# Attention queries transposed by VectorE from 32 by 32 blocks in SBUF, keys still by TensorE

## The chip, the cores and the metric

One core of one Trainium2 chip. The metric is the device time in microseconds of one execution. "Time" below is the median of some executions; each profile is of one of them, and its span is about 2 us shorter than its time. "Fast" is the usual state of an execution.

## The reference

Two stages, cut to what matters. 64 heads of attention with a threshold, then one feed-forward layer over the joined heads:

```python
# q, k, v: (8, 8, 576, 64) float32; tau = 0.02
scores = q @ k.T / 8                                  # per head, 576 x 576
thresh = max(scores, -1) - tau
scores = where(scores >= thresh, scores, -1e9)
attn = softmax(scores)
x = (attn @ v), heads joined                          # (4608, 512)
h = x @ w_in                                          # (4608, 2048)
g = h * clip(h + 3, 0, 6) / 6
out = g @ w_out                                       # (4608, 512) float32
```

## The kernel before

A main loop of 16 quads (four heads, as two pairs) times nine slots. A slot is 128 query rows of two heads. PSUM is the memory that TensorE's results go to here, SBUF the one that the operands are kept in; to evict is to copy a result from PSUM to SBUF, which makes the PSUM buffer free for its next user. In the same slots run the feed-forward matmuls of earlier batches. Heads of a pair stand one below the other, 64 partitions each, so scores need queries and keys as [2 x 64, 576]; both are brought there by transposes.

```python
ps_s = psum_pool(bufs=2)   # scores      ps_h = psum_pool(bufs=1)  # x @ w_in
ps_o = psum_pool(bufs=1)   # g @ w_out   ps_m = psum_pool(bufs=1)  # transposes AND attn @ v

def transpose_main(pair, i):                       # i = 0: queries, 1: keys
    main = nat[pair // 2][i][0]
    ps = ps_m.tile([P, 512], F32, tag="m", name="tp")
    for t in range(4):
        nc.tensor.transpose(ps[:, t * P:(t + 1) * P], main[:, t, 2 * (pair % 2):2 * (pair % 2) + 2, :], identf[:])
    def evict():
        if i == 0:
            nc.scalar.activation(out=qkT[pair][0][:, 0:512], in_=ps[:], func=Act.Copy, scale=scale)
        else:
            nc.scalar.copy(out=qkT[pair][1][:, 64:576], in_=ps[:])
    return evict
# ... transpose_rest: the last 64 rows of q and k, the same way, in four small transposes

def av_main(pair):                                 # attn @ v for 512 rows: the same ps_m
    ps = ps_m.tile([P, 512], F32, tag="m", name="av")
    # ... ten matmuls
    nc.vector.tensor_copy(out=xT[b][:, hp, o0:o0 + 512], in_=ps[:])
```

The order of issue in one slot follows. In the traces the engines take up their work in this order:

```python
        sm_exp(prev, 0); sm_exp(prev, 1)           # ScalarE, the slot before
        sm_max(sl)                                 # VectorE: 2 passes over the scores; GpSimd: bias
        if slot != 8 and todo1:
            h = mm1(i, j)                          # TensorE
            r = mm1_relu(h, on_act=(slot in (0, 3)))   # ScalarE in two slots, VectorE in the others
            mm1_gate(i, j, h, r)                   # VectorE, waits for r
        sm_recip(prev)                             # VectorE
        # ... some of the g @ w_out matmuls, evicted by VectorE
        sm_mask(sl, 0); sm_mask(sl, 1)             # ScalarE
        if slot in (1, 2):    evict = transpose_main(2 * quad + 1, slot - 1)
        elif slot == 3:       av_main(2 * quad - 1)        # if quad > 0
        elif slot == 4:       av_rest(quad - 1)            # if quad > 0
        elif slot in (5, 6):  evict = transpose_main(nxt, slot - 5)
        elif slot == 7:       evict = transpose_rest((nxt, nxt + 1))
        elif slot == 8:       av_main(2 * quad)
        if evict: evict()                          # ScalarE, behind the slot's two masks
        queue[n + 1].tiles = scores(...)           # TensorE
        sm_norm(prev)                              # GpSimd, then a DMA transpose of the probabilities
```

## Time and profile before

| | before |
|---|---|
| median time | 592.41 us (592.33 to 594.22, 3 runs) |
| first reciprocal of VectorE | 15.6 us |
| first four quads together | 123.2 us (30.8 each) |
| the next eleven quads | 32.97 us each |
| TensorE busy, 60 to 90 us / 300 to 350 us | 25.15 of 30 / 50.00 of 50 |

The quads are timed by VectorE's reciprocals in the trace: nine a quad, one a slot, and the distance from the first of one quad to the first of the next is that quad's pace. This divides the span into a start, an early part in which the feed-forward work has hardly begun (its ReLUs start at 87 us), a middle, and a tail. The lines of the profile are in the prediction below.

### The profile page before, as it was taken

To read this page: it belongs to the slowest core of one execution; us is meant where nothing else is said; L and a number is where in the kernel's file an instruction comes from. 1 tells how busy PE (TensorE), PEld (TensorE's weight loads), DVE (VectorE), ACT (ScalarE), POOL (GpSimd) and SP (SyncE) were. 2 spreads that over 40 slices of the span, in tenths; PEclk is the share of its full clock that TensorE was granted. 3 is DMA by queue.
4 is the path that set the end of the run, shared out by engine and by line. 5 is a ranking of instruction groups with operands and counts; after the bars stand their busy time and mean duration, and the time that the engine had idled before them with its cause. 6 is when DMAs were issued, how large, how long until landed. Compare 5 with 4: busy or idle time off the path is not lost. (4 is left out here: it accounts for less than half of the span.)

```text
span 589.8 us, 11554 instructions
## 1 busy us (share of the span) xinstructions
PE 552.3 (94%) x3840; PEld 319.8 (54%) x3840; DVE 412.4 (70%) x1008; ACT 480.0 (81%) x1078; POOL 305.5 (52%) x646
## 2 busy tenths in 40 slices
PE   6887698889999999999999999999999999999997
PEld 3544354545556555656556565655556565554663
DVE  1545467777878887888868787888868787872350
ACT  4999899798889898898878988898879989881340
POOL 0769676875555555654555555654555555550000
PEclk9978689989999999999999999999999999999999
DMA  5999999999697768976697758985698746552101
GB/s 116 142 178 191 180 152 192 163 177 154 132 154 150 154 119 152 152 155 137 140 137 155 151 119 163 141 162 126 133 138 158 153 101 108 97 110 69 54 19 71
DMA packets 269498, 80.45 MB, mean 136 GB/s; under 512 B 252544, under 2 KB 264832, under 8 KB 269440
## 3 DMA queue, kind: packets, MB, share of 16 engines
q1 hardware_dynamic: 252032, 70.81, 63.4%
q0 software_dynamic: 17408, 8.92, 13.5%
q8 instruction: 30, 0.49, 0.4%
q14 instruction: 28, 0.23, 0.1%
HBM read 36.70 MB, written 9.44 MB: 78 GB/s over the span
## 5 line engine op out<-in xcount | busy, mean ns | idle before, releaser
L230 POOL TENSOR_SCALAR pn<-s,rinv 128x576 bf16<-128x576 f32 x288 | 211.6, 745 | 143.8 <-issue 89.3
L210 DVE TENSOR_SCALAR_CACHE_REDUCE s<-s 128x576 f32<-128x576 f32 x288 | 206.7, 755 | 86.6 <-PE s L189 69.1
L218 ACT ACTIVATE s<-s,bias 128x576 f32<-128x576 f32 x288 | 207.3, 767 | 56.1 <-POOL bias L213 55.3
L222 ACT ACTIVATE s<-s 128x576 f32<-128x576 f32 x288 | 192.9, 672 | 0.4
L189 PE MATMUL s<-kT,qT 64*128 64x288 f32 x1024 | 178.2, 450 | 3.4 <-DVE s L210 2.3
L274 PE MATMUL h<-xT,w_in_sb 128*128 128x288 bf16 x1024 | 144.6, 287 | 3.5 <-DVE g L290 2.8
L302 PE MATMUL o<-w_out_sb,g 128*128 128x512 bf16 x576 | 139.9, 379 | 3.9 <-DVE osb L310 3.9
L274 PEld LDWEIGHTS <-w_in_sb 128*128 128x128 bf16 x1024 | 91.6, 98 | 65.8 <-issue 21.1
L189 PEld LDWEIGHTS s<-kT,qT 64*128 64x128 f32 x1024 | 98.6, 195 | 49.7 <-DVE s L210 12.8
L290 DVE SCALAR_TENSOR_TENSOR g<-r,h 128x576 bf16<-128x576 f32 x128 | 96.5, 754 | 26.1 <-ACT r L282 23.3
L213 POOL TENSOR_SCALAR bias<-m 128x1 f32<-128x1 f32 x288 | 54.6, 190 | 79.0 <-DVE s L210 58.3
L302 PEld LDWEIGHTS <-g 128*128 128x128 bf16 x576 | 55.6, 98 | 59.6 <-issue 9.9
L284 DVE TENSOR_SCALAR r<-h 128x576 f32<-128x576 f32 x81 | 61.0, 753 | 0.0
L222 ACT ACTIVATION_READ_ACCUMULATOR s<-s 128x1 f32 x288 | 54.4, 189 | 0.0
L282 ACT ACTIVATE r<-h,three 128x576 f32<-128x576 f32 x47 | 34.5, 736 | 12.3 <-PE h L274 11.8
L245 PE MATMUL av<-pT,vm 128*64 128x512 bf16 x256 | 36.0, 405 | 8.0 <-ACT kT L174 6.3
L310 DVE TENSOR_SCALAR osb<-o 128x512 f32<-128x512 f32 x30 | 20.3, 678 | 29.3 <-PE o L302 28.6
L245 PEld LDWEIGHTS <-vm 128*64 128x64 bf16 x512 | 20.3, 112 | 33.5 <-issue 26.8
L225 DVE RECIPROCAL rinv<-rsum 128x2 f32<-128x2 f32 x144 | 23.0, 160 | 21.2 <-ACT s L222 20.8
L308 ACT ACTIVATE osb<-o 128x512 f32<-128x512 f32 x6 | 3.6, 597 | 30.4 <-PE o L302 30.4
L152 PE MATMUL tp<-identf,km 128*128 128x128 f32 x128 | 20.9, 288 | 7.1 <-ACT qT L156 7.1
L258 DVE CAST xT<-av 128x512 bf16<-128x512 f32 x32 | 21.8, 682 | 6.3 <-PE av L249 6.3
(32 smaller groups left out, 270.5 us busy)
## 6 DMA issues: line engine op xcount, KB each, us to landing
qm<-in_q_dram SPq DMA_DIRECT2D x64, 128.0 KB, 3.1
km<-in_k_dram SPq DMA_DIRECT2D x64, 128.0 KB, 3.0
out_dram<-osb SPq DMA_DIRECT2D x32, 256.0 KB, 2.6
vm<-in_v_dram POOLq DMA_DIRECT2D x16, 256.0 KB, 5.9
pT<-pn SPq DMA_TRANSPOSE x128, 3.5
w_in_sb<-in_moe_w_in_dram POOLq DMA_DIRECT2D x16, 128.0 KB, 4.1
w_out_sb<-in_moe_w_out_dram POOLq DMA_DIRECT2D x16, 128.0 KB, 3.6
qr<-in_q_dram SPq DMA_DIRECT2D x16, 64.0 KB, 2.7
```

What stands on the lines that cost most here:

```text
L189: nc.tensor.matmul(tiles[a][:, hf, 0:HALF], qkT[pair][0][a * 64:(a + 1) * 64, t * P:(t + 1) * P], keys(pair, a, hf), start=True, stop=True)
L210: nc.vector.tensor_scalar(out=sl.s[:, i, :].rearrange("p (a b) -> p a b", a=2), in0=ps[:, :, 0:HALF], scalar1=1.0, scalar2=None, op0=Alu.m ...
L213: nc.gpsimd.tensor_scalar(out=sl.bias[:, i:i + 1], in0=sl.m[:, i:i + 1], scalar1=-1.0, scalar2=tau, op0=Alu.mult, op1=Alu.add)
L218: nc.scalar.activation(out=s, in_=s, func=Act.Prelu, bias=sl.bias[:, i:i + 1], alpha=REJECT)
L222: nc.scalar.activation(out=s, in_=s, func=Act.Exp, accum_out=sl.rsum[:, i:i + 1])
L230: nc.gpsimd.tensor_scalar(out=pn[:, i, :], in0=sl.s[:, i, :], scalar1=sl.rinv[:, i:i + 1], scalar2=1.0, op0=Alu.mult, op1=Alu.mult)
L245: nc.tensor.matmul(ps[a * 64:(a + 1) * 64, :], vm[:, 2 * hp + a, c * D:(c + 1) * D], pT[:, 5 * a + c, cols], start=(c == 0), stop=False)
L274: nc.tensor.matmul(hps[:, hf, 0:HALF], w_in_sb[:, ki, ni * P:(ni + 1) * P], xT[b][:, ki, hf * HALF:(hf + 1) * HALF], start=(ki == 0), stop ...
L282: nc.scalar.activation(out=r[:], in_=hps[:, :, 0:HALF], func=Act.Relu, bias=three[:])
L284: nc.vector.tensor_scalar(out=r[:], in0=hps[:, :, 0:HALF], scalar1=3.0, scalar2=0.0, op0=Alu.add, op1=Alu.max)
L290: nc.vector.scalar_tensor_tensor(out=g.rearrange("p (a b) -> p a b", a=2), in0=r[:], scalar=6.0, in1=hps[:, :, 0:HALF], op0=Alu.min, op1=A ...
L302: nc.tensor.matmul(o_ps[0], gbuf[:, ni, mt * P:(mt + 1) * P], w_out_sb[:, ni, :], start=(ni == 0), stop=(ni == NI - 1))
```

## The change

Intent: take 160 transposes of the queries and their evictions off TensorE and ScalarE. Each 32-wide half of a head is loaded on its own 32 partitions, so that VectorE's transposition of 32 by 32 blocks gives the wanted layout, from SBUF to SBUF. The scale of 1/8 goes from the eviction into the mask, and ScalarE takes over two more ReLUs a quad from VectorE. Query rows are in plain order now, so the rows of the output are too. The diff, with the change of the loops' bookkeeping cut:

```diff
     def load_quad(quad):
+        nat[quad] = (nat_pool.tile([P, 2, 18, 32], F32, tag="nq", name="nq"),
+                     nat_pool.tile([P, 4, 4, D], F32, tag="km", name="km"), ...)
+        def main_q(n, a, j):
+            c = 32 * (2 * a + j)
+            nc.sync.dma_start(out=nat[quad][0][c:c + 32, n, :, :],
+                              in_=q[b, 4 * g + 2 * n + a, :, 32 * j:32 * j + 32].rearrange("(k r) d -> r k d", r=32))
@@
+    def transpose_q(pair):
+        nc.vector.transpose(out=qkT[pair][0][:], in_=nat[pair // 2][0][:, pair % 2, :, :].rearrange("p k d -> p (k d)"))
+    def transpose_k(pair):      # as transpose_main with i = 1
@@ transpose_rest
-            for i in range(2):
-                nc.tensor.transpose(ps[:, (2 * n + i) * 64:(2 * n + i + 1) * 64], ...)
+            nc.tensor.transpose(ps[:, n * 64:(n + 1) * 64], nat[pair // 2][2][:, 2 * n:2 * n + 2, :], identf[:64, :64])
@@ sm_max, sm_mask
-            ... bias: scalar1=-1.0, scalar2=tau
+            ... bias: scalar1=-scale, scalar2=tau
-        nc.scalar.activation(out=s, in_=s, func=Act.Prelu, bias=sl.bias[:, i:i + 1], alpha=REJECT)
+        nc.scalar.activation(out=s, in_=s, func=Act.Prelu, bias=sl.bias[:, i:i + 1], scale=scale, alpha=REJECT)
@@ mm2_out
-        return [(osb[:], out[r0:r0 + 512, :].rearrange("(p t) n -> p t n", t=4)[:, t, :])]
+        return [(osb[:], out[r0 + t * P:r0 + (t + 1) * P, :])]
@@ main loop
-            r = mm1_relu(h, on_act=(slot in (0, 3)))
+            r = mm1_relu(h, on_act=(slot in (0, 1, 3, 5)))
-        if slot in (1, 2):
-            evict = transpose_main(2 * quad + 1, slot - 1)
+        if slot == 1:
+            transpose_q(2 * quad + 1)
+        elif slot == 2:
+            evict = transpose_k(2 * quad + 1)
@@ slot 5
-            evict = transpose_main(nxt, slot - 5) if slot < 7 else transpose_rest((nxt, nxt + 1))
+                transpose_q(nxt)
+            elif slot == 6:
+                evict = transpose_k(nxt)
+            else:
+                evict = transpose_rest((nxt, nxt + 1))
```

More of the change, by code (lines that the diff above doesn't have):

```diff
@@ L76, in load_quad, with main_k, rest @@
         b, g = divmod(quad, 2)
-        nat[quad] = []
-        for nm in "qk":
-            nat[quad].append((nat_pool.tile([P, 4, 4, D], F32, tag=nm + "m", name=nm + "m"),
-                              nat_pool.tile([64, 4, D], F32, tag=nm + "r", name=nm + "r")))
-        def main(i, h):
-            src = (q, k)[i]
-            nc.sync.dma_start(out=nat[quad][i][0][:, :, h, :],
-                              in_=src[b, 4 * g + h, 0:512, :].rearrange("(p t) d -> p t d", t=4))
-        def rest(i):
-            src = (q, k)[i]
-            nc.sync.dma_start(out=nat[quad][i][1][:],
-                              in_=src[b, 4 * g:4 * g + 4, 512:S, :].rearrange("h p d -> p h d"))
+        nat[quad] = (nat_pool.tile([P, 2, 18, 32], F32, tag="nq", name="nq"),
+                     nat_pool.tile([P, 4, 4, D], F32, tag="km", name="km"),
+                     nat_pool.tile([64, 4, D], F32, tag="kr", name="kr"))
+        def main_q(n, a, j):
+            c = 32 * (2 * a + j)
+            nc.sync.dma_start(out=nat[quad][0][c:c + 32, n, :, :],
+                              in_=q[b, 4 * g + 2 * n + a, :, 32 * j:32 * j + 32].rearrange("(k r) d -> r k d", r=32))
+        def main_k(h):
+            nc.sync.dma_start(out=nat[quad][1][:, :, h, :],
+                              in_=k[b, 4 * g + h, 0:512, :].rearrange("(p t) d -> p t d", t=4))
+        def rest():
+            nc.sync.dma_start(out=nat[quad][2][:],
+                              in_=k[b, 4 * g:4 * g + 4, 512:S, :].rearrange("h p d -> p h d"))
         for n in range(2):
-            for i in range(2):
-                loads.append(lambda n=n, i=i: [main(i, 2 * n + a) for a in range(2)])
+            loads.append(lambda n=n: [main_k(2 * n + a) for a in range(2)])
+            loads.append(lambda n=n: [main_q(n, a, j) for a in range(2) for j in range(2)])
             if n == 0:
-                loads.append(lambda: [rest(i) for i in range(2)])
+                loads.append(rest)
     def load_v(b):
@@ L146, in alloc_qk @@
                      qk_pool.tile([P, S + 64], F32, tag="kT", name="kT"))
-    def transpose_main(pair, i):
-        main = nat[pair // 2][i][0]
+    def transpose_q(pair):
+        nc.vector.transpose(out=qkT[pair][0][:], in_=nat[pair // 2][0][:, pair % 2, :, :].rearrange("p k d -> p (k d)"))
+    def transpose_k(pair):
         ps = ps_m.tile([P, 512], F32, tag="m", name="tp")
         for t in range(4):
-            nc.tensor.transpose(ps[:, t * P:(t + 1) * P], main[:, t, 2 * (pair % 2):2 * (pair % 2) + 2, :], identf[:])
-        def evict():
-            if i == 0:
-                nc.scalar.activation(out=qkT[pair][0][:, 0:512], in_=ps[:], func=Act.Copy, scale=scale)
-            else:
-                nc.scalar.copy(out=qkT[pair][1][:, 64:576], in_=ps[:])
-        return evict
+            nc.tensor.transpose(ps[:, t * P:(t + 1) * P],
+                                nat[pair // 2][1][:, t, 2 * (pair % 2):2 * (pair % 2) + 2, :], identf[:])
+        return lambda: nc.scalar.copy(out=qkT[pair][1][:, 64:576], in_=ps[:])
     def transpose_rest(pairs):
@@ L163, in transpose_rest @@
         for n, pair in enumerate(pairs):
-            for i in range(2):
-                nc.tensor.transpose(ps[:, (2 * n + i) * 64:(2 * n + i + 1) * 64],
-                                    nat[pair // 2][i][1][:, 2 * n:2 * n + 2, :], identf[:64, :64])
+            nc.tensor.transpose(ps[:, n * 64:(n + 1) * 64], nat[pair // 2][2][:, 2 * n:2 * n + 2, :], identf[:64, :64])
         def evict():
             for n, pair in enumerate(pairs):
-                qT, kT = qkT[pair]
-                src = ps[:, 2 * n * 64:(2 * n + 1) * 64], ps[:, (2 * n + 1) * 64:(2 * n + 2) * 64]
-                nc.scalar.activation(out=qT[:, 512:S], in_=src[0], func=Act.Copy, scale=scale)
-                nc.scalar.copy(out=kT[0:64, S:S + 64], in_=src[1][0:64, :])
-                nc.scalar.copy(out=kT[64:P, 0:64], in_=src[1][64:P, :])
+                kT = qkT[pair][1]
+                nc.scalar.copy(out=kT[0:64, S:S + 64], in_=ps[0:64, n * 64:(n + 1) * 64])
+                nc.scalar.copy(out=kT[64:P, 0:64], in_=ps[64:P, n * 64:(n + 1) * 64])
         return evict
@@ L212, in sm_max @@
                                     accum_out=sl.m[:, i:i + 1])
-            nc.gpsimd.tensor_scalar(out=sl.bias[:, i:i + 1], in0=sl.m[:, i:i + 1], scalar1=-1.0, scalar2=tau,
+            nc.gpsimd.tensor_scalar(out=sl.bias[:, i:i + 1], in0=sl.m[:, i:i + 1], scalar1=-scale, scalar2=tau,
                                     op0=Alu.mult, op1=Alu.add)
@@ L217, in sm_mask @@
         s = sl.s[:, i, :]
-        nc.scalar.activation(out=s, in_=s, func=Act.Prelu, bias=sl.bias[:, i:i + 1], alpha=REJECT)
+        nc.scalar.activation(out=s, in_=s, func=Act.Prelu, bias=sl.bias[:, i:i + 1], scale=scale,
+                             alpha=REJECT)
     def sm_exp(sl, i):
@@ L332 @@
     alloc_qk(1)
-    for i in range(2):
-        transpose_main(0, i)()
+    transpose_q(0)
+    transpose_k(0)()
     transpose_rest((0, 1))()
```

## The prediction

> **What bounds the kernel now.** I read the engines' busy shares first, then stretches of the span, then the waits of the long middle part, and last the order of time within single slots. (A slot is one pass of the main loop, 128 query rows of two heads; nine slots make a quad of four heads; there are 16 quads.) The engines, and TensorE's row and granted clock over 40 slices:
>
> ```profile
> PE 552.3 (94%) x3840; PEld 319.8 (54%) x3840; DVE 412.4 (70%) x1008; ACT 480.0 (81%) x1078; POOL 305.5 (52%) x646
> ...
> PE   6887698889999999999999999999999999999997
> ...
> PEclk9978689989999999999999999999999999999999
> ```
>
> TensorE is full from the tenth slice on and not before; there its clock is also reduced. The stretches show the same with numbers (columns: stretch, length, then busy us of PE, PEld, DVE, ACT, POOL, clock, DMA share, GB/s):
>
> ```profile
> 60.00:90.00 30.00, 25.15 (x152) 14.20 (x151) 16.45 (x49) 27.04 (x63) 19.79 (x43) 0.77 1.05 166
> ...
> 300.00:350.00 50.00, 50.00 (x374) 29.62 (x374) 41.13 (x100) 42.95 (x96) 26.35 (x57) 1.00 0.77 136
> ```
>
> So there are two regimes and a tail: quads 0 to 3 (to about 140 us), where ScalarE is busiest and TensorE waits; quads 4 to 15 (to 530 us), where TensorE does nothing but work; and about 60 us of feed-forward matmuls alone, which the change does not touch. A busy TensorE need not be a limiting one, so I asked who waits for whom between 165 and 500 us:
>
> ```profile
> PE o L302 <- DVE osb L310: 3.7, 5, 1.4
> ...
> ACT s L218 <- POOL bias L213: 38.5, 56, 2.2
> ...
> DVE s L210 <- PE s L189: 39.8, 57, 2.4
> ```
>
> In 335 us TensorE waits 4.3 us in all (the row shown and one of 0.6), while VectorE waits 39.8 us for TensorE's scores and ScalarE 38.5 us for what follows from them. This middle is TensorE's, and what is taken off TensorE there shortens it. The pace is read from the once-per-quad transpose of the leftover probabilities:
>
> ```profile
> 137.78 1.51 SPq L237 DMA_TRANSPOSE pR<-pn  x1
> ...
> 498.93 1.30 SPq L237 DMA_TRANSPOSE pR<-pn  x1
> ```
>
> Eleven quads in 361.2 us are 32.8 us each; the three before took (137.8 - 43.0)/3 = 31.6 us.
>
> [...] The new load puts each 32-wide half of a head on its own 32 partitions, so that blocks are enough and no eviction follows. [...] I estimate 0.75 us. The trace agrees for passes of that size (753 to 755 ns for 128x576 in f32), but no transpose is in it. [...] in the 0.77 stretch a slot's eight score matmuls took 2.29 us, against 1.24 us later.
>
> **The change, part by part.** The rows concerned:
>
> ```profile
> L284 DVE TENSOR_SCALAR r<-h 128x576 f32<-128x576 f32 x81 | 61.0, 753 | 0.0
> ...
> L282 ACT ACTIVATE r<-h,three 128x576 f32<-128x576 f32 x47 | 34.5, 736 | 12.3 <-PE h L274 11.8
> ...
> L152 PE MATMUL tp<-identf,qm 128*128 128x128 f32 x128 | 20.9, 289 | 4.5 <-DMA qm<-in_q_dram 4.5
> ...
> L156 ACT ACTIVATE qT<-tp 128x512 f32<-128x512 f32 x32 | 18.5, 578 | 3.7 <-PE tp L152 3.6
> ...
> L172 ACT ACTIVATE qT<-tr 128x64 f32<-128x64 f32 x32 | 6.8, 213 | 1.0 <-PE tr L165 0.8
> ```
>
> *TensorE.* 128 query transposes and the 32 small ones go. Their 20.9 + 6.7 us of busy time overlap with neighbours, so I take the pitch from the order of time: a group of four stands between the last output matmuls and the next scores,
>
> ```profile
> 349.23 0.60 PE L152 MATMUL tp<-identf,qm 128*128 128x128 f32 x4
> ...
> 349.75 1.24 PE L189 MATMUL s<-kT,qT 64*128 64x288 f32 x8
> ```
>
> which is 0.52 us; the four small transposes take 0.39 us in the same way, so the two of the queries 0.19. Per quad: 2 x 0.52 + 0.19 = **1.23 us** of TensorE's own time, all on the path in the middle.
>
> *ScalarE.* It loses 32 evictions of 578 ns and 32 of 213 ns, 25.3 us, and takes over ReLUs: built, the changed kernel has 74 on ScalarE for 47, 27 x 0.736 = 19.9 us. Each one replaces a query eviction in its slot (the second and the sixth), so ScalarE's load stays. From the order of time its pitch in a slot is 1.34 us for the two masks and 1.35 for the two exponentials, plus 0.62 for a ReLU or 0.47 for an eviction. A quad is then 9 x 2.69 + 4 x 0.62 + 2 x 0.47 + 0.8 = 28.4 us. In the second and sixth slot it is 3.31 us against TensorE's 3.56 - 0.52 = 3.04, but the neighbouring slots give it back.
>
> *VectorE.* 27 ReLUs of 753 ns leave (-20.3 us), 32 transposes of an estimated 0.75 us come (+24.0). Per quad, with issue pitches of 0.68 (a maximum pass), 0.67 (gate), 0.74 (ReLU) and so on: 12.3 + 1.4 + 5.4 + 3.0 + 3.0 (casts and outputs) + 1.5 (transposes) = 26.6 us. The gate waits for a ReLU on ScalarE: in the middle 11.9 us over 10.2 quads with two such slots, 0.58 us each, so four make 2.3 us: 28.9 us of TensorE's new 31.6. It stays under, but close: in the second and sixth slot the transpose stands between the gate and the next maximum, some 0.3 us later than TensorE would have the scores, 0.9 where an output is evicted as well. I take off 0.25 us per quad.
>
> *Transfers.* The queries arrive in pieces of 128 B for 256 B. Between 2 and 13 us only such loads run: 6880 packets, 68.6% of 16 engines for 11 us, so 17.5 ns a packet of 256 B. A quad's queries were 2304 packets, 40 us of engine time, and become 4608. [...] at an unchanged price per packet 81 us; [...] the queue stands thus:
>
> ```profile
> q1 hardware_dynamic: 252032, 70.81, 63.4%
> ```
>
> The loads are asked for a quad ahead and the transposed probabilities three slots (10 us) ahead of a landing of 3.5 us, so I count nothing for it in the middle.
>
> *First four quads.* ScalarE loses its query evictions with nothing in their place (no ReLU runs before 86 us). And one PSUM buffer serves all transposes, so the key transposes wait for the query eviction:
>
> ```profile
> PEld tp L152 <- ACT qT L156: 10.6, 8, 2.3
> ```
>
> That wait vanishes. Two evictions of 0.47 and two of about 0.2 are 1.3 us a quad, the wait some 2.6 us in a quad, partly the same time; I estimate 1.75 us a quad.
>
> *Sum.* Twelve quads x (1.23 - 0.25) = 11.8 us; four x 1.75 = 7.0; start and tail 0. 592.4 - 18.8 = **573.6 us**. The scale moved into the mask's instruction and the changed order of output rows cost nothing: same passes, same 2 KB rows.
>
> **The rivals.** First, *VectorE takes over as the bound*: [...] most of the middle's gain goes: about 582 us. For it: VectorE is already the engine that ScalarE and TensorE hand over to; against: 39.8 us in which it waited for TensorE. Second, *transfers become the bound early*: the DMA share is 1.05 in the stretch from 60 us before anything is added. If the price per packet stays, 2.5 us more per quad could cancel the early gain, about 580 us. Against: none of TensorE's long waits there names a transfer. Third, *the clock*: with the transposes gone TensorE is emptier in the first quads and may be slowed more; a slot whose scores take 2.29 us in place of 1.24 costs a microsecond, and eight more such slots would take 8 us, again about 581. Fourth, the good case: the first quads fall to ScalarE's own pace (9 x 2.69 + 1.7 = 26 us for 31.6), worth up to 15 us more, about 562.
>
> **Range and chances.** The middle's 12 us I trust to 4 us, the early 7 us only to -7 and +8. Range 564 to 582. Faster by 2% means below 580.6. Each of the first three rivals alone lands near that line, two of them together cross it: 0.82 for faster, 0.16 for within 2%, 0.02 for slower.
>
> **What would show it.** TensorE: 1.2 us less per quad, the pace from 138 to 499 us at 31.6 to 32.0 us, TensorE still above 96% busy there, waits below 12 us. VectorE: 32 transposes of 0.7 to 0.8 us; over 1.1 us makes the first rival true. The wait of key transposes for a query eviction gone, the first three intervals at 29 to 31 us. Loads: a landing of 3 to 5 us and no wait of VectorE's transposes for one after the start. It is wrong if TensorE's waits in the middle rise by more than 12 us in all, if the early clock falls below 0.75, or if the quad's pace does not move.

Beside it, from the trace of the kernel before: TensorE's granted clock was 0.50 where the eight score matmuls took 2.29 us (from 68.34 us) and 1.00 where they took 1.24 (from 349.75 us); in the same early stretch those of other slots took 1.24 and 1.91. The 0.75 us for a transpose on VectorE is the estimate, with passes of the same size (753 to 755 ns) to go by. The 81 us of engine time, against 40 and over 16 engines, are the 2.5 us per quad that the second rival names; that the price of 17.5 ns a packet would stay was an assumption. The 582 us of the first rival are an estimate too: no trace before the change has a transpose of VectorE in it.

## The result, and the profile after

**584.78 us** (median of 4 runs, 583.45 to 585.68) against 592.89 us for the kernel before in its four runs: 8.1 us less, where 18.8 had been predicted, and outside the range of 564 to 582. The outputs are right. The ratio is 0.9858, 95% interval 0.983 to 0.9886, so the change is within 2%, to which the prediction had given a chance of 0.16. Such ratios, here and below, are the mean time of one kernel's fast runs over that of the other's of the same rounds, so not quite the ratio of the medians that are quoted.

The page of the kernel after: the engines, the rows of TensorE and of its granted clock over 40 slices, and the queue of the loads.

```profile
PE 541.4 (93%) x3642; PEld 308.2 (53%) x3680; DVE 411.4 (71%) x1013; ACT 477.6 (82%) x1041; POOL 305.5 (52%) x646
...
PE   5877798879999999999989999999989999999997
...
PEclk9797778998999999999999999999999999999999
...
q1 hardware_dynamic: 289664, 70.81, 65.8%
```

TensorE has about 11 us less work and the early slices are no fuller. VectorE's and ScalarE's loads stayed, as worked out. The groups that changed (busy us, mean ns of one, idle time before):

```profile
L280 ACT ACTIVATE r<-h,three 128x576 f32<-128x576 f32 x74 | 54.3, 735 | 29.3 <-PE h L272 28.7
...
L282 DVE TENSOR_SCALAR r<-h 128x576 f32<-128x576 f32 x54 | 40.7, 753 | 0.0
...
L153 DVE STREAM_TRANSPOSE qT<-nq 128x576 f32<-128x576 f32 x32 | 24.4, 762 | 5.7 <-DMA nq<-in_q_dram 5.6
```

The two stretches of the prediction, after the change:

```profile
60.00:90.00 30.00, 25.12 (x141) 13.98 (x138) 16.49 (x48) 26.42 (x61) 19.87 (x43) 0.72 1.10 165
300.00:350.00 50.00, 49.74 (x365) 28.68 (x368) 42.20 (x104) 45.03 (x98) 27.59 (x59) 1.00 0.81 143
```

And the pace, by the same once-per-quad transposes:

```profile
139.86 1.32 SPq L235 DMA_TRANSPOSE pR<-pn  x1
...
493.62 1.29 SPq L235 DMA_TRANSPOSE pR<-pn  x1
```

Eleven quads in 353.8 us, 32.16 each. But the first of these two lines comes at 139.86 us, 2.1 us *later* than before. The spans of the two traces, divided by the reciprocals, differ as follows (the spans differ by 6.3 us; the runs' medians, from more executions, by 8.1):

| | before | after | gain, us | predicted |
|---|---|---|---|---|
| start, to the first reciprocal | 15.56 | 14.18 | +1.4 | 0 |
| quads 0 and 1 | 59.76 | 60.67 | -0.9 | +3.5 |
| quads 2 and 3 | 63.43 | 66.38 | -2.95 | +3.5 |
| quads 4 to 14, each | 32.97 | 32.22 | +0.75 x 11 = +8.2 | +0.98 x 11 |
| quad 15 and tail | | | -0.2 and +0.8 | +1.0 and 0 |
| sum | | | 6.3 | 18.8 |

So there are two gaps: most of it is in the first four quads (7.0 predicted, -3.9 came), a smaller one in the middle.

**The early waits.** The list of waits from 45 to 75 us (who waited for whom: us, times, longest), before:

```profile
PE tp L152 <- ACT qT L156: 2.8, 2, 1.9
...
PE av L245 <- ACT kT L174: 2.0, 1, 2.0
...
PE av L245 <- ACT kT L158: 0.7, 1, 0.7
```

and after:

```profile
PE av L243 <- ACT kT L160: 2.8, 1, 2.8
PE av L243 <- ACT kT L171: 2.0, 1, 2.0
```

The wait of the key transposes for the eviction of the queries is gone. But the value matmuls go through the same PSUM buffer, and now wait 2.8 us, where it was 0.7, for the eviction of the *keys* (L160, before L158). Their other wait of 2.0 us, for the keys' last rows, was there before. Why the eviction of the keys is late is seen in the order of time around it (start, duration, engine, operation, in brackets the wait and what ended it):

```profile
46.38 1.44 ACT L215 ACTIVATE s<-s,bias 128x576 f32<-128x576 f32 x2 [0.61 <-POOL bias L210]
...
47.85 0.58 ACT L160 COPY kT<-tp 128x512 f32<-128x512 f32 x1
...
48.49 1.92 PE L243 MATMUL av<-pT,vm 128*64 128x512 bf16 x8 [2.84 <-ACT kT L160]
```

ScalarE evicts only behind the two masks of the slot, which themselves wait for the maximum and the bias. TensorE waits for the buffer longer than before.

This is one window. Over the whole early part, 14 to 140 us, TensorE's matmuls waited as follows, in us, in the two profiles of each kernel (the second ones are r_before and r_after, at the end of the experiments):

| waited for | before | after |
|---|---|---|
| query evictions (the key transposes) | 5.9, 7.8 | 0, 0 |
| key evictions (the value matmuls) | 7.8, 7.3 | 10.5, 9.2 |
| VectorE's maxima (the scores) | 2.3, 3.1 | 5.5, 7.2 |
| VectorE's gate (the feed-forward) | 0.9, 1.4 | 3.6, 3.9 |
| all waits | 20.0, 20.4 | 21.4, 20.6 |

So TensorE's waiting stayed what it was in all. What the query evictions had cost came back in three places, a quarter to a half of it at the keys' evictions and the rest at VectorE. ScalarE, with fewer evictions to do, waited longer for the bias instead: 13.6 and 12.2 us for 9.3 and 8.4.

**The ReLUs.** In the first four quads ScalarE had 3 ReLUs before and has 7 after, and VectorE's gate waited 3.0 us for them before and 8.7 us after. In the middle (165 to 500 us), where the prediction counted four of them a quad, the same wait was, before:

```profile
DVE g L290 <- ACT r L282: 11.9, 21, 1.5
```

and the waits after:

```profile
DVE s L207 <- PE s L186: 27.1, 36, 2.4
DVE g L288 <- ACT r L280: 20.3, 42, 1.6
ACT s L215 <- POOL bias L210: 17.4, 39, 1.4
...
PE o L300 <- DVE osb L308: 4.6, 5, 1.7
```

with one further wait of TensorE, of 1.5 us. VectorE and ScalarE have lost a good part of their slack, and in some slots the order of time shows TensorE's scores ready before VectorE is:

```profile
315.74 1.24 PE L186 MATMUL s<-kT,qT 64*128 64x288 f32 x8
315.97 0.75 DVE L288 SCALAR_TENSOR_TENSOR g<-r,h 128x576 bf16<-128x576 f32 x1 [0.43 <-ACT r L280]
...
316.72 0.76 DVE L153 STREAM_TRANSPOSE qT<-nq 128x576 f32<-128x576 f32 x1
...
317.40 0.72 DVE L207 TENSOR_SCALAR_CACHE_REDUCE s<-s 128x576 f32<-128x576 f32 x1
```

The scores end at 316.98; the gate has waited 0.43 us for its ReLU, the transpose follows, and the maximum starts at 317.40.

### The profile page after: what moved, and what is told of

The parts are those of the page before. It is cut to its first block, busy times and chain, and to the rows that moved or that the text cites. A ratio compares the mean times of both kernels' runs of the same rounds, so it can differ in the third digit from the quotient of the medians.

```text
span 583.5 us, 11270 instructions
## 1 busy us (share of the span) xinstructions
PE 541.4 (93%) x3642; PEld 308.2 (53%) x3680; DVE 411.4 (71%) x1013; ACT 477.6 (82%) x1041; POOL 305.5 (52%) x646
## 3 DMA queue, kind: packets, MB, share of 16 engines
q1 hardware_dynamic: 289664, 70.81, 65.8%
## 5 line engine op out<-in xcount | busy, mean ns | idle before, releaser
L186 PE MATMUL s<-kT,qT 64*128 64x288 f32 x1024 | 187.4, 460 | 5.6 <-DVE s L207 5.3
L300 PE MATMUL o<-w_out_sb,g 128*128 128x512 bf16 x538 | 132.8, 379 | 7.1 <-DVE osb L308 5.0
L186 PEld LDWEIGHTS s<-kT,qT 64*128 64x128 f32 x1024 | 104.7, 199 | 61.9 <-DVE s L207 29.1
L272 PEld LDWEIGHTS <-w_in_sb 128*128 128x128 bf16 x1024 | 92.2, 98 | 71.1 <-issue 33.8
L300 PEld LDWEIGHTS <-g 128*128 128x128 bf16 x576 | 55.5, 98 | 60.8 <-issue 11.0
L280 ACT ACTIVATE r<-h,three 128x576 f32<-128x576 f32 x74 | 54.3, 735 | 29.3 <-PE h L272 28.7
L308 DVE TENSOR_SCALAR osb<-o 128x512 f32<-128x512 f32 x30 | 20.3, 678 | 29.0 <-PE o L300 28.6
L282 DVE TENSOR_SCALAR r<-h 128x576 f32<-128x576 f32 x54 | 40.7, 753 | 0.0
L153 DVE STREAM_TRANSPOSE qT<-nq 128x576 f32<-128x576 f32 x32 | 24.4, 762 | 5.7 <-DMA nq<-in_q_dram 5.6
```

What stands on the lines that cost most here:

```text
L186: nc.tensor.matmul(tiles[a][:, hf, 0:HALF], qkT[pair][0][a * 64:(a + 1) * 64, t * P:(t + 1) * P], keys(pair, a, hf), start=True, stop=True)
L272: nc.tensor.matmul(hps[:, hf, 0:HALF], w_in_sb[:, ki, ni * P:(ni + 1) * P], xT[b][:, ki, hf * HALF:(hf + 1) * HALF], start=(ki == 0), stop ...
L280: nc.scalar.activation(out=r[:], in_=hps[:, :, 0:HALF], func=Act.Relu, bias=three[:])
L282: nc.vector.tensor_scalar(out=r[:], in0=hps[:, :, 0:HALF], scalar1=3.0, scalar2=0.0, op0=Alu.add, op1=Alu.max)
L300: nc.tensor.matmul(o_ps[0], gbuf[:, ni, mt * P:(mt + 1) * P], w_out_sb[:, ni, :], start=(ni == 0), stop=(ni == NI - 1))
```

## The experiments

Theories for the early part: (a) TensorE, emptier, is given a lower clock (0.72 against 0.77 at 60 to 90 us), (b) the 128-byte pieces of the loads slow the transfers, (c) the single PSUM buffer passes the wait on to the keys' eviction, (d) the ReLUs moved to ScalarE cost more there than they save. For the middle: (e) the transpose on VectorE stands on the path.

The early and middle paces of all profiled runs, from the reciprocals. Two looks at one kernel differ by up to 1.2 us in a pair of early quads or in quad 3. But e5 and e16, which are the same program in the first four quads, differ by 1.2 us in the first pair, 2.2 in the second and 3.3 in all four. So a difference of up to some 3 us in the first four quads of two profiles says nothing by itself. The middle repeats within 0.01 us.

| run | quads 0-1 | quads 2-3 | quad 3 alone | middle, each |
|---|---|---|---|---|
| before, two looks | 59.8, 58.8 | 63.4, 64.3 | 33.2, 32.0 | 32.97, 32.97 |
| after, two looks | 60.7, 60.2 | 66.4, 65.5 | 34.0, 34.1 | 32.22, 32.23 |
| e1_same_work | 61.1 | 66.4 | 34.1 | 32.23 |
| e2_filler | 61.8 | 64.8 | 33.3 | 32.23 |
| e3_coarse_loads | 59.7 | 66.4 | 34.0 | 32.23 |
| e4_hoist | 60.6 | 64.9 | 32.6 | 32.22 |
| e5_relu_back | 60.2 | 63.0 | 31.9 | 32.59 |
| e6_twice | 57.7 | 68.9 | 34.8 | 33.24 |
| e7_before_filler | 57.9 | 67.0 | 33.4 | 32.97 |
| e10_dve_evict | 58.8 | 65.8 | 33.3 | 32.23 |
| e11_no_weight_loads | 59.1 | 65.0 | 34.0 | 32.18 |
| e12_before_no_weight_loads | 57.6 | 64.2 | 33.2 | 32.94 |
| e13_third | 60.8 | 63.6 | 33.6 | 32.06 |
| e14_combined | 57.6 | 66.2 | 33.8 | 32.05 |
| e15_combined_no_weights | 54.4 | 59.6 | 31.1 | 32.0 |
| e16_relu_early | 61.4 | 65.2 | 32.4 | 32.23 |

All times below are medians of four runs, against the kernel before in the same rounds (592.1 to 592.6 us in the four groups of runs).

### The clock: e1, e2, e7

e1 gives TensorE its eight query transposes a quad back in the first four quads, into a buffer that nobody waits for:

```diff
+        if slot in (1, 5) and quad < 4:
+            idle = ps_o.tile([P, d_model], F32, tag="o", name="idle")
+            for t in range(4):
+                nc.tensor.transpose(idle[:, t * P:(t + 1) * P], identf[:], identf[:])
```

> The changed kernel, with the removed query transposes of TensorE put back as empty work in the first four quads only (two groups of four a quad, written to an unused PSUM bank, read by nobody; no eviction on ScalarE). Clock theory (the first quads lost their gain because an emptier TensorE is slowed): the clock from 15 to 90 us rises from 0.72-0.88 towards the 0.77-1.00 of before, and the first four quads (127 us from the first to the fifth quad after, 123 before) come back to 121-124 us, so 580 to 583 us in all. Transfer theory: no change or slightly slower, 584 to 587. ScalarE-eviction theory (TensorE waits for the late key evictions, whatever it does meanwhile): unchanged within 1 us, clock a little higher.

Measured: 583.84 us, ratio 0.9846 (0.982 to 0.9873); first four quads 127.4 us against 127.0 after, with a clock of 0.77 for 0.72 at 60 to 90 us. TensorE's missing work is not the reason.

e2 fills more, four matmuls of 512 columns in every slot of the first four quads; e7 does the same to the kernel before.

```diff
+        if quad < 4:
+            idle = ps_o.tile([P, d_model], F32, tag="o", name="idle")
+            for _ in range(4):
+                nc.tensor.matmul(idle[:], zb[:, 0:P], zb[:], start=True, stop=True)
```

> The changed kernel, with four empty bf16 matmuls of 128x512 (about 0.9 us at full clock) after the scores of every slot of the first four quads. Clock theory: clock 0.95 or more from 30 to 140 us, first four quads at 116-122 us for 127, in all 574 to 580. If only the work counts and not the clock: four quads slower by up to 36 x 0.9 us where TensorE is the limit, 590 or more. Transfer theory: no gain, 584 to 588.

> The kernel before, with the same empty matmuls as in the second run in its first four quads. Clock theory: its early clock rises to 0.95 or more and its first four quads get shorter, 118-121 us for 123, in all 588 to 591. If the clock is not what limits the first quads: 124 us or more there, 593 to 597.

Four matmuls of 128x512 in bf16 take 0.87 us of TensorE's line in the trace of before (348.36 to 349.23 us, in a stretch with a clock of 1.00).

Measured: e2 586.01 us, ratio 0.9892 (0.9866 to 0.9918). The stretch from 60 to 90 us of e2:

```profile
60.00:90.00 30.00, 29.29 (x183) 15.26 (x186) 18.53 (x56) 27.93 (x63) 21.81 (x47) 0.97 1.18 169
```

and of e7, 594.13 us, ratio 1.0026 (0.9992 to 1.006):

```profile
60.00:90.00 30.00, 26.40 (x179) 13.91 (x183) 16.68 (x49) 28.15 (x68) 20.06 (x45) 1.00 1.21 185
```

The clock came up from 0.72 to 0.97, and in e7 from 0.77 to 1.00, and the first four quads took 126.6 and 124.8 us: no gain for either kernel. The filling takes TensorE's own time too and could hide a small gain, but e5 and e16 below, with nothing filled in and the same early program, have a clock of 0.88 and 0.92 in the first four quads, and the one with the higher clock is the slower by 3.3 us. **Theory (a) falls.** The clock was higher where TensorE was given more to do (0.97 with 29.29 of 30 us busy in e2, 0.72 with 25.12 after), though not only there (1.00 with 25.70 in e15, below), and the pace didn't follow it. e2 also uncovered, for 3.3 us, a wait of the value matmuls for a DMA transpose that had not landed: something else stands right behind.

### The loads: e3

The queries are loaded in 256-byte pieces as before, with the same bytes, and land in places where the transposes give nonsense: wrong (relative error 1.34).

```diff
         def main_q(n, a, j):
+            if j == 0:      # one load per head, "(p t) d -> p t d" as the keys
+                nc.sync.dma_start(out=<the same tile, seen as p t h d>[:, :, h, :], in_=q[b, 4 * g + h, 0:512, :]...)
+            elif a == 1 and n == 0:      # the last rows of all four heads
+                nc.sync.dma_start(out=..., in_=q[b, 4 * g:4 * g + 2, 448:S, :]...)
```

> Wrong result on purpose: the changed kernel with the queries loaded in the old 256-byte pieces (as many packets as before) into the same tile, so VectorE's transposes and all else stay. Transfer theory: the first four quads return to 120-123 us, DMA share of the first 150 us falls by 0.05 to 0.1, in all 577 to 581. Clock theory and eviction theory: 583 to 586 (start up to 1.5 us later, because the first transpose then waits for both pairs).

Measured: 586.88 us, ratio 0.9902 (0.9877 to 0.9926). The first four quads took 126.1 us for 127.0, and the start is 3.2 us later (1.5 had been allowed for), because the first transpose then has to wait for loads that cover both pairs. Without this later start the time would be 583.7 us for 584.8, so piece size is worth about 1 us, where the theory asked for 4 or more. **Theory (b), granularity by itself, falls.** The price is there: the queue's share of 16 engines times the span was 0.634 x 16 x 589.8 = 5983 us before and 0.658 x 16 x 583.5 = 6143 us after, 10 us of engine time more per quad. The runs show nothing on the path that waits for it.

### Where the transposes stand on VectorE: e4, e6, e13

e4 issues them before the gate instead of behind it, directly behind the maximum:

```diff
         sm_max(sl)
+        if slot == 1:
+            transpose_q(2 * quad + 1)
+        elif slot == 5 and quad + 1 < NQUAD:
+            alloc_qk(2 * quad + 2); alloc_qk(2 * quad + 3)
+            transpose_q(2 * quad + 2)
```

> The changed kernel with VectorE's transpose moved ahead: right after the maximum passes of its slot, in the time in which the gate waits for ScalarE's ReLU. If the place of the transpose in VectorE's order costs the middle its missing 0.3 us per quad (0.75 measured, 1.0 expected): 0.2 to 0.4 us less per quad from 140 to 524 us, in all 580 to 582.5. If it costs nothing because TensorE is limited by the gate after ScalarE's ReLU: within 1 us of 584.8, or slower where the gate comes later.

e6 does each transpose twice, e13 only a third of it (192 columns of 576; scores reuse those: wrong).

```diff
# e6: the line of transpose_q a second time
# e13:
-        nc.vector.transpose(out=qkT[pair][0][:], in_=nat[pair // 2][0][:, pair % 2, :, :]...)
+        nc.vector.transpose(out=qkT[pair][0][:, 0:192], in_=nat[pair // 2][0][:, pair % 2, 0:6, :]...)
```

> The changed kernel with every VectorE transpose done twice (right result): 32 more of 0.76 us. If VectorE's transposes lie on the path: 2 x 0.76 us more per quad, 24 us in all, about 608. If VectorE has room for them in the middle (27 us waited for scores in 335 us there): less than 6 us more, 585 to 590.

> Wrong result on purpose: the changed kernel with only the first third of each query tile transposed (128x192, some 0.33 us for 0.76) and every score matmul reading from that third, so TensorE, ScalarE and transfers are as they were. If VectorE's transposes lie on the path in the middle (doubling them cost 0.85 to 1.3 us a quad): 0.25 to 0.5 us less per quad, 31.7 to 31.9 for 32.2, in all 579 to 582. If only a second one tips over the edge: under 0.1 us a quad, 583 to 585.

Measured: e4 584.34 us, ratio 0.9865 (0.9843 to 0.9887); e6 597.86, 1.0088 (1.0059 to 1.0117); e13 580.09, 0.9796 (0.9749 to 0.9843). The third of a transpose in the groups of e13, 363 ns where some 0.33 us had been expected:

```profile
L153 DVE STREAM_TRANSPOSE qT<-nq 128x192 f32<-128x192 f32 x32 | 11.6, 363 | 5.7 <-DMA nq<-in_q_dram 5.6
```

Two of them a quad save 2 x (762 - 363) = 0.8 us of VectorE, and the middle's pace fell by 0.16 us. Twice the transposes add 1.5 us and cost 1.02. So a transpose of this length is hidden for the most part, and there is no room for a second one. (Both paces lie between the two cases that had been expected.) **Theory (e) holds in small part**: the transposes account for 0.16 us, or 0.24 if the whole of one goes as two thirds do (an estimate from e13), of the 0.48 us by which the middle's pace misses TensorE's own saving of 1.23. That 1.23 is itself worked out from an order of time and was tested by no run, so a part of the 0.48 may be a saving that was never there. Moving them alone (e4) brought nothing in the middle, 32.22. A change there that no experiment took up: from 165 to 500 us the weight loads of the scores waited 0.2 us for VectorE's maxima before and 10.2 after, and still 9.0 in e13.

### The ReLUs: e5, e16

e5 gives VectorE its ReLUs back everywhere, e16 in the first four quads only.

```diff
-            r = mm1_relu(h, on_act=(slot in (0, 1, 3, 5)))
+            r = mm1_relu(h, on_act=(slot in (0, 3)))                                        # e5
+            r = mm1_relu(h, on_act=(slot in ((0, 3) if quad < 4 else (0, 1, 3, 5))))        # e16
```

> The changed kernel with ReLUs on ScalarE only in the first and fourth slot, as before the change (so 27 more on VectorE). If the moved ReLUs cost the third and fourth quad their 3 us (63.4 us before, 66.4 after, for both) and the middle its missing 0.25 us per quad: those two quads at 63 to 65 us, middle 31.5 us per quad, in all 578 to 582. If they were needed to make room for the transposes on VectorE (a slot then holds two maxima, ReLU, gate and transpose, 3.7 us of VectorE against 3.1 of TensorE): 586 to 592.

> The changed kernel, with the ReLUs of the second and sixth slot on VectorE in the first four quads only (as before the change) and on ScalarE later. If ScalarE's ReLU in the slot of VectorE's transpose is what costs the third and fourth quad 3 us: those two at 62.5 to 64 us for 66.4, the middle unchanged at 32.2 a quad, in all 581 to 582.5. If not: 65.5 to 67 us and 584 to 585.5.

Measured: e5 586.65 us, ratio 0.991 (0.9887 to 0.9934); e16 584.68, 0.9867 (0.9838 to 0.9897). Quad 3 went from 34.0 to 31.9 us in e5 and to 32.4 in e16: **theory (d) is supported for quad 3**, where undoing the move brought 1.6 to 2.1 us, against 34.0 to 34.1 in five profiles (after, its second, e1, e3, e11). But e4 takes quad 3 to 32.6 with the ReLUs left on ScalarE and only the transposes moved, and the kernel before has 33.2 and 32.0, so it is not shown that the ReLUs alone are the cause. In the middle it is the other way: e5 loses 0.37 us a quad, and TensorE's weight loads wait there for VectorE, which they did for 4.4 us after the change:

```profile
PEld L272 <- DVE g L288: 16.7, 36, 0.7
```

e16 as a whole is a miss. It had been expected to bring quads 2 and 3 to 62.5 to 64 us and they took 65.2. Quad 3 did as expected, while in quad 2 one slot took 6.0 us (4.1 in e5), with TensorE's weight loads waiting 2.1 and 1.5 us for DMA transposes. That is one run's trace; the three other executions (583.05 to 584.83 us) show no gain over the kernel after either.

### The handover: e10

In the early quads the keys are evicted by VectorE, which is not behind ScalarE's masks.

```diff
+        copy = nc.vector.tensor_copy if 0 < pair < 8 else nc.scalar.copy
-        return lambda: nc.scalar.copy(out=qkT[pair][1][:, 64:576], in_=ps[:])
+        return lambda: copy(out=qkT[pair][1][:, 64:576], in_=ps[:])
# the two small evictions of transpose_rest in the same way, for 1 < pair < 8
```

> The changed kernel with the key evictions of the first four quads moved from ScalarE to VectorE (same PSUM buffer, same sizes; ScalarE in the rest). Handover theory (in the first quads TensorE's wait for a query eviction became a wait for the key eviction that ScalarE does only after the slot's masks, so nothing was gained): that wait of the probability-times-value matmuls falls below 1 us in all, the first four quads from 127 to 118-122 us, in all 576 to 580. If ScalarE's ReLUs or the transfers set the pace of the first quads: 583 to 586. If VectorE takes over as the limit there: 586 to 590.

Measured: 581.56 us, ratio 0.982 (0.9785 to 0.9855). The wait of the value matmuls for the keys at 45 to 75 us, 2.8 and 2.0 us after the change, became

```profile
PE av L245 <- DVE kT L161: 1.0, 1, 1.0
```

and from 14 to 140 us the value matmuls waited 3.1 us for the keys in all, for 10.5 and 9.2. The first four quads took 124.6 us for 127.0 and 125.8, within their spread, and the time is 2 to 3 us less. **Theory (c) is supported, for about 2 to 3 us**, though by this run alone not beyond doubt: its interval overlaps that of the change (0.983 to 0.9886). As a forecast it missed: 118 to 122 us and 576 to 580 had been expected if the handover were all. TensorE's waiting in the early part is again 20.3 us: 7.6 us of it now for VectorE's maxima. And the next wait appears, in the list of 75 to 107 us:

```profile
PE ar L245 <- DMA pR<-pn: 2.3, 1, 2.3
```

### The transfers behind it: e11, e12, e14, e15

e11 (from after) and e12 (from before) don't load the feed-forward weights but set them to a constant, by GpSimd; wrong (relative error 4.8).

```diff
-                casts.append(lambda ...: nc.gpsimd.dma_start(out=w_in_sb[:, ki, n4 * 512:(n4 + 1) * 512], in_=moe_w_in[...]))
+                casts.append(lambda ...: nc.gpsimd.memset(w_in_sb[:, ki, n4 * 512:(n4 + 1) * 512], 0.01))
# w_out_sb likewise
```

> Wrong result on purpose: the changed kernel with the 32 weight transfers of the first five quads replaced by GpSimd filling the same tiles, 128x512 in each of the same places. If what is left of the first quads' pace is transfers (the weights' queue takes up to 39% of the 16 engines there and the transposed probabilities land late, as the last runs' waits for them hint): the first four quads at 112-118 us for 127, their transposes landing in 3.5 to 4.5 us for 5, in all 570 to 578. If transfers do not matter there: 124-127 us and 582 to 586.

> Wrong result on purpose: the same replacement in the kernel before. With the run above it shows what the change is worth in the first quads without the weights' traffic. If the handover through ScalarE is what limits both: 118-123 us for 123, and the changed kernel's gain there, against this one, is 0 to 3 us. If transfers hid a gain: this one 119-122, the changed one 5 to 8 us less.

Measured: e11 582.16 us, ratio 0.9837 (0.9798 to 0.9877); e12 590.88, 0.9983 (0.9945 to 1.002). 32 loads of 128 KB fewer bring the first four quads from 127.0 and 125.8 us (two looks) to 124.1 in the one kernel, and from 123.2 to 121.8 in the other, little in both. The queue q0, which brings the weights and the values, took 38.2% of 16 engines from 30 to 60 us after. The weights were in the way of the other transfers: the DMA transposes of the first four quads landed in 5.2 us after (median of 32) and in 3.6 in e11, in 4.8 before and 3.3 in e12. But as long as the buffer was waited for, landing sooner brought next to nothing.

e14 puts together what had helped or done no harm: e4's and e10's edits, and ScalarE's ReLUs at other slots. e15 is e14 with e11's edit, and wrong for it.

```diff
# e4's and e10's edits, and
-            r = mm1_relu(h, on_act=(slot in (0, 1, 3, 5)))
+            r = mm1_relu(h, on_act=(slot in (0, 1, 4, 5)))
# e15: e11's edit as well
```

> A correct candidate: the changed kernel with VectorE's transpose right after its slot's maxima, the early key evictions on VectorE (first four quads), and ScalarE's fourth ReLU moved from the fourth slot, which follows a key eviction, to the fifth, which has none. If ScalarE's late ReLU in the fourth slot is the rest of the middle's loss: 31.6 to 31.9 us a quad for 32.2, with the early evictions 576 to 580 in all. If the fourth slot needs it (VectorE copies the values there as well): 32.2 to 32.6 us a quad, 581 to 585.

> Wrong result on purpose: the combined version (576.5 us) without the weight transfers. In its profile TensorE waited 3 us each time for the transposed probabilities in the first quads (landing 5 to 8 us). If transfers are what then limits: no such wait, landing 3.5 to 4.5 us, first four quads at 112-117 us for 123.8, in all 566 to 572. If something else holds them: 120-124 us and 574 to 578.

Measured: **e14 576.51 us** (575.23 to 580.41), correct, ratio 0.975 (0.9699 to 0.98), the fastest correct version, below the interval of the change. e15: 572.59 us, 0.9669 (0.9632 to 0.9706). TensorE's waits in e14, from 45 to 75 us,

```profile
PE ar L245 <- DMA pR<-pn: 3.1, 1, 3.1
```

from 75 to 107 us,

```profile
PE av L245 <- DMA pT<-pn: 3.4, 1, 3.4
```

and from 107 to 140 us

```profile
PE ar L245 <- DMA pR<-pn: 3.0, 1, 3.0
```

The handover's wait has given way to three waits for transposed probabilities, 9.5 us together. The landing of the first of them, in e14 at 44 to 58 us (times, us from issue to landing):

```profile
pR<-pn SPq DMA_TRANSPOSE x1, 8.3
```

From 14 to 140 us the median landing is 5.3 us in e14 and 3.5 in e15. In e15 the stretch from 60 to 90 us has a DMA share of 0.83 (the last column but one, the time that the packets took as a share of 16 engines' time, so that it can exceed 1; it was 1.19 in e14), and TensorE's clock is 1.00, for 0.90 in e14:

```profile
60.00:90.00 30.00, 25.70 (x180) 14.30 (x180) 25.09 (x73) 28.62 (x64) 23.43 (x51) 1.00 0.83 149
```

Its first four quads took 113.9 us, against 123.8 in e14. This difference is too large to be typical: e14's profiled run was the slowest of its four (580.41 us), e15's the fastest (569.97). The medians, 576.51 and 572.59, put it at 4 us, and the ratios, 0.975 and 0.9669, at 0.0081 x 592 = 4.8, though their intervals just touch. By the ratios the same loads were worth 1.0 us in e12 and, against the change's 0.9858, 1.2 us in e11. So they seem to be worth more once the handover is out of the way; with intervals that touch, this is likely and not shown beyond doubt. The reading that fits all these runs is that **two limits lie one behind the other**: the single PSUM buffer, then transfers while the weights come (a DMA share of 1.19 from 60 to 90 us in e14, 0.83 without the weights in e15). Removing the first one alone shows little (2 to 3 us, e10), and removing the second alone as well (1.0 us in e12, 1.2 in e11).

In the middle e14 has a pace of 32.05 us, where 31.6 to 31.9 had been expected, and the gate's wait for ScalarE from 165 to 500 us is down from 20.3 us:

```profile
DVE g L290 <- ACT r L282: 7.9, 20, 0.6
```

### Second looks: r_before and r_after

Both kernels unchanged, once more, on the chip of the last group.

> The kernel before once more, for a second profile: how far its first two quads (59.8 us in the first profile) and its third and fourth (63.4) vary from run to run. If they are as steady as the middle: within 0.5 us.

> The changed kernel once more, for the same reason: first two quads 60.7 us and third and fourth 66.4 in the first profile. If steady: within 0.5 us; if the first two vary by 2 us or more, their difference of 0.9 between the kernels is not to be explained.

Measured: 591.94 and 584.12 us; first four quads 123.1 and 125.8 us. The early part is again the longer one after the change, by 2.7 us for 3.9. With a spread of 3.3 us between e5 and e16 it is certain that the predicted 7 us didn't come, and not that anything was lost: the medians of all runs (8.1 us), less what the middle, the start and the tail gave, leave some 2 us of loss. The waits agree: the keys' evictions held the value matmuls for 2.9 us at 45 to 75 us after, while before it was 1.4 and the query evictions held the key transposes for 3.3.

## Why the prediction was wrong, and where it was right

Right, by the prediction's own tests:

- *The transposes*: 32 of them, median 758 ns, for 0.75 estimated.
- *The middle is TensorE's*: it stayed full (49.74 of 50 us), its waits there were 4.6 + 1.5 = 6.1 us, below the 12 that would have refuted this.
- *Loads*: landing in 3.0 us; VectorE's transposes waited for a load once, 5.6 us, at the start.
- *The wait of key transposes for the query eviction* is gone.
- *The scale in the mask and the changed order of output rows* cost nothing to be seen: a mask took 767 ns before and 766 after in the mean, and the 256 KB output transfers landed in 2.6 and 2.4 us.
- *Two of the rivals failed as they should*: VectorE did not become the bound. The clock did fall, to 0.72, below the 0.75 that was named as what would make the prediction wrong, but e1, e2 and e16 speak against it as a cause.

Wrong:

- **The step that failed is "First four quads"**: "ScalarE loses its query evictions with nothing in their place" and "That wait vanishes", 1.75 us a quad, 7.0 in the sum. Measured: -3.9 us, and -2.7 in the second look, so this term alone is 9.7 to 10.9 us too large, for a gain that fell 10.7 us short in all (the middle's shortfall, below, is about balanced by the start, the tail and the spread of the runs). Two things were missed. First, the evictions and the wait were counted as if they lay on the path. The wait did vanish (5.9 and 7.8 us of the matmuls' time, to 0), but TensorE's matmuls waited as long as before in all, 21.4 and 20.6 us for 20.0 and 20.4: 2.7 and 1.9 us more for the keys' evictions, which use the same single buffer behind ScalarE's masks, 3.2 and 4.1 more for VectorE's maxima, 2.7 and 2.5 more for its gate. And ScalarE spent the time that it had won waiting for the bias, some 4 us more. (The line from which the prediction read "some 2.6 us in a quad" is that of the weight loads over the whole run; the matmuls waited 5.9 us in the early part, 1.5 a quad.) That the keys' evictions are a part of it is supported by e10 (2 to 3 us); what VectorE's maxima contribute was tested by no run. Secondly, "no ReLU runs before 86 us" was right and covers only half of the four quads: from 87 us on ReLUs do come, and ScalarE has 7 for 3 there; undoing it gives quad 3 some 2 us back (e5, e16), though e16 as a whole gained nothing. And behind both stood transfers, which would probably have taken up a part of the gain (e14, e15).
- *The middle*, right in mechanism and off in size: "(1.23 - 0.25)" = 0.98 a quad was 0.75, so 0.48 is lost for 0.25. Either the 1.23 was too large, which was not tested, or the term for VectorE too small: e13, with a third of the transposes, won 0.16 a quad, and e14, with ReLUs in other slots, 0.17. 8.2 us came of 10.8 in eleven quads.
- *Start and tail*, counted 0, gave 1.4 and 0.8 us, which hid a part of the miss. That is luck; why was not pursued.
- *Transfers* as second rival: the piece size was harmless (e3), yet transfers are, as far as e14 and e15 show, the next limit. The argument against, "none of TensorE's long waits there names a transfer", was no argument: the waits for transfers came up only when others were removed (0 us after, 9.5 in e14). Nor did the price per packet stay: that would have been some 40 us of engine time more per quad, and 10 came (e3's section).

What stays open: quads 0 and 1, without any ReLU, took 0.9 and 1.4 us longer in the two pairs of looks. With a spread of 1.2 us between two profiles of the same early program that may be the handover or nothing. Some kernels (e6, e7) took 57.7 and 57.9 us there and then 68.9 and 67.0 in quads 2 and 3: the sum of all four (126.6 and 124.8) differs less from the other runs than its parts do, and why it is shared out so differently was not found. How much of the 0.3 us a quad that e14 still leaves in the middle belongs to the ReLUs, to the weight loads' waiting for VectorE, to transfers or to a saving of less than 1.23, was not separated.

## What to carry to other kernels

When work leaves a buffer that several users hand around, look at who comes next to it: with one buffer and an engine that evicts only behind other work, a part of the wait can turn up at the next user and the rest at another engine, as here, where the sum of TensorE's early waits was 20.0 and 20.4 us before and 21.4 and 20.6 after. A gain there should be counted only after following one full round of the buffer. A list of waits can leave out a limit that lies behind another one: here the DMA share was 1.05 before and 1.10 after from 60 to 90 us, and transfers were a candidate although TensorE waited 0 us for them after (9.5 in e14). A part of a loop should be estimated for its own mixture of work: the start had a different one than the middle, and an exchange of work between two engines that helps in the one cost in the other (the ReLUs on ScalarE: undoing it in e5 cost 0.37 us a quad in the middle and quad 3 was 2.1 us shorter).

## Figures of the hardware that the runs show

- A transpose on VectorE in f32 took 762 ns for 128x576 in the trace after and 363 for 128x192 in e13 (means), a difference of 399 ns for 384 columns. From these two an estimate is 1.04 ns a column and 0.16 us beside it.
- A group of four f32 128x128 transposes on TensorE takes 0.52 us of its line in the trace of before, 0.13 each, though each instruction is shown with 289 ns. The prediction counted the 0.52; what taking them out saves was not tested by itself.
- Filling TensorE raised the granted clock at 60 to 90 us from 0.72 to 0.97 (e2) and left the first four quads at 126.6 us for 127.0: here a higher clock brought nothing.
- With 128-byte pieces for the queries the queue of the loads had 289664 packets for 252032 and took 10 us of engine time more per quad. The DMA transposes of the first four quads landed in 5.2 us as the median of the kernel after and 3.6 without the weights' loads (e11), and one in e14 in 8.3 us.
- With one PSUM buffer that several users share while ScalarE evicts it, 5.9 and 7.8 us of waiting for it were removed, and 2.7 and 1.9 us came back at its next user.
